# Strided attention heads as 72-token slices, two-bank MLP accumulators and reordered first transfers in a fused attention and MLP kernel

## The chip, the cores and the metric

The kernel runs on one core of a Trainium2 chip. The metric is the device time of one execution in microseconds; before the change the median of three runs is 445.27 us (444.51 to 446.03).

## The reference

Eight batches of attention with 8 heads over 576 tokens of 64 features, then an MLP on the 4608 tokens of 512 features:

```python
scores = scale * np.matmul(q, k.transpose(0, 1, 3, 2))
rel = pos[:, None] - pos[None, :]
mask_local = (rel >= 0) & (rel < stride)                       # heads 0 to 3, stride = 32
mask_strided = (rel >= 0) & (pos[None, :] % stride == pos[:, None] % stride)  # heads 4 to 7
...
attn = np.exp(scores)
attn = attn / (np.sum(attn, axis=-1, keepdims=True) + 1e-09)
...
x = np.ascontiguousarray(attn_out.transpose(0, 2, 1, 3)).reshape(B * S, H * D)
...
h = x @ w_in
sp = np.where(h > 20.0, h, np.log1p(np.exp(np.minimum(h, 20.0))))
g = h * np.tanh(sp)
return (g @ w_out).astype(np.float32)
```

A local head's token sees the 32 tokens up to itself; a strided head's token sees the tokens at distance 0, 32, 64 and so on behind it.

## The kernel before

Q, K and V come from HBM in float32 through one queue (SyncE's), are cast to bf16 (by GpSimd, for batch 0 partly by VectorE), and Q and K are transposed by TensorE, so that features lie on partitions (`t_steps`, L144: eight steps a batch, five transposes each, four of 128 tokens and one of 64). Scores are computed keys by queries: for local heads in windows of 96 queries against 128 keys (`qk_local`, L183), for strided heads in tiles of 7 residues of 18 tokens, 126 by 126, and a last one of 4 residues, 72 by 72 (`qk_str`, L203, `qk_str4`, L224). The copies behind the transposes put the strided tokens in residue order (L162, L166). ScalarE takes the exponential from PSUM into one of six tiles P, and GpSimd multiplies it with a mask (L197, L219, L238). The output steps (`pv_local`, `pv_str`) multiply P with V, to which a column of ones is appended, and VectorE divides by the sum that this column gives (`norm`, L243: a reciprocal and a product). The result is transposed back (`xt_local`, `xt_str`) into x^T, `xT`, which holds all 4608 tokens.

The MLP works in nine blocks of 512 tokens. Block t has a first half, `mlp1` (16 groups of four 512-column matmuls, each followed by Mish on ScalarE into gT), and a second half, `mlp2` (16 groups of four matmuls, four groups to each 128-token output tile; then a copy by VectorE and a store). A block's tokens lie in batch t and the batch before, so the attention of batch t + 1 is written in between the groups of block t: its transposes in the first half, its scores, outputs and x^T in the second, one step behind each group. All engines work in the order of the program; nothing is reordered later.

PSUM has eight banks: three single ones for MLP accumulators, a pair for scores, one for outputs, two for transposes. Loads, casts and attention of different batches overlap: at block t the program issues the casts of batch t + 2, then the loads of batch t + 3. On GpSimd the casts of batch t + 2 therefore stand ahead of the masks of batch t + 1 (L408 to L410 against L424). Each float32 landing tile exists once, so a load waits for the casts of the batch before it. The strided half of V is loaded by 20 transfers a batch, one per head and tile (L112 to L118). At the start SyncE issues K, Q, the constants and V of batch 0; w_in and w_out go through GpSimd's software queue, which casts to bf16 on the way.

Of the kernel before, what the change touches and what calls it, by code (L numbers as in the profile page):

```python
# [10 lines left out]
F32 = mybir.dt.float32  # L11
# [7 lines left out]
RG = 7  # L19
NA = 18  # L20
NTS = 5


def _masks():
    kk = np.arange(128)[:, None]
    qq = np.arange(WQ)[None, :]
    rel = qq + 32 - kk
    band = (rel >= 0) & (rel < STRIDE)
    loc = np.stack([band & (kk >= 32)] + [band] * (NW - 1), axis=1).astype(np.float32)

# [14 lines left out]
def kernel(ctx, tc, q, k, v, moe_w_in, moe_w_out, out):  # L45
# [19 lines left out]
    xT = const.tile([128, 4, NT], BF16, name="xT")  # L65
    loc = const.tile([128, NW, WQ], BF16, name="loc")
    m7 = const.tile([128, 126], BF16, name="m7")
    m4 = const.tile([128, 72], BF16, name="m4")
    ident = const.tile([128, 128], BF16, name="ident_sb")
    q32 = const.tile([128, 5, H, D], F32, name="q32")  # L70
    k32 = const.tile([128, 5, H, D], F32, name="k32")
    vl32 = const.tile([128, NW, 4, D], F32, name="vl32")
    vs32 = const.tile([128, NTS, 4, D], F32, name="vs32")
    qbf = [const.tile([128, 5, H, D], BF16, name=f"qbf{i}") for i in range(2)]
    kbf = [const.tile([128, 5, H, D], BF16, name=f"kbf{i}") for i in range(2)]
    vl = [const.tile([128, NW, 4, D + 1], BF16, name=f"vl{i}") for i in range(2)]
    vs = [const.tile([128, NTS, 4, D + 1], BF16, name=f"vs{i}") for i in range(2)]
    qTl = const.tile([128, 2, S], BF16, name="qTl")
    kTl = const.tile([128, 2, 32 + S], BF16, name="kTl")
    qTs = const.tile([128, 2, S], BF16, name="qTs")  # L80
    kTs = const.tile([128, 2, 640], BF16, name="kTs")
    NP = 6
    P = [const.tile([128, 2, 320], BF16, name=f"P{i}") for i in range(NP)]
    x_l = const.tile([128, NW, 256], BF16, name="x_l")
    x_s = const.tile([128, NTS, 256], BF16, name="x_s")
# [5 lines left out]
    ps_mm = ctx.enter_context(tc.tile_pool(name="psmm", bufs=3, space=PS))  # L91
    ps_s = ctx.enter_context(tc.tile_pool(name="pss", bufs=1, space=PS))
    ps_o = ctx.enter_context(tc.tile_pool(name="pso", bufs=1, space=PS))
    ps_t = ctx.enter_context(tc.tile_pool(name="pst", bufs=2, space=PS))


    def load_qk(b, dst, src):
        for kb in range(5):
            n = 128 if kb < 4 else 64
            nc.sync.dma_start(  # L100
                dst[0:n, kb, :, :],
                src[b, :, 128 * kb:128 * kb + n, :].rearrange("h p d -> p h d"),
            )
# [22 lines left out]
    def cast_qk(b, engs):  # L126
        for src, dst in ((q32, qbf[b % 2]), (k32, kbf[b % 2])):
            e = next(engs)
            cast(e, dst[:, 0:2, :, :], src[:, 0:2, :, :])
            cast(e, dst[:, 2:4, :, :], src[:, 2:4, :, :])  # L130
            cast(e, dst[0:64, 4, :, :], src[0:64, 4, :, :])

    def cast_v(b, engs):
        for i in range(0, NW, 3):
            cast(next(engs), vl[b % 2][:, i:i + 3, :, 0:D], vl32[:, i:i + 3, :, :])
        cast(next(engs), vs[b % 2][:, 0:4, :, 0:D], vs32[:, 0:4, :, :])
        cast(next(engs), vs[b % 2][0:72, 4, :, 0:D], vs32[0:72, 4, :, :])

    def forever(*es):
        while True:  # L140
            yield from es


    def t_steps(b):  # L144

        def step(which, hp):
            src = (qbf if which == "q" else kbf)[b % 2]
            tr = ps_t.tile([128, 1024], BF16, tag="tr", name="tr")
            for kb in range(5):
                n = 128 if kb < 4 else 64  # L150
                nc.tensor.transpose(  # L151
                    tr[:, 128 * kb:128 * kb + n],
                    src[0:n, kb, 2 * hp:2 * hp + 2, :],
                    ident[0:n, 0:n],
                )
            if hp < 2:
                dst = qTl[:, hp, :] if which == "q" else kTl[:, hp, 32:32 + S]
                nc.vector.tensor_copy(dst, tr[:, 0:S])
            else:
                dst = (qTs if which == "q" else kTs)[:, hp - 2, :]  # L160
                nat = tr[:, 0:S].rearrange("p (a r) -> p a r", r=32)
                nc.vector.tensor_copy(  # L162
                    dst[:, 0:504].rearrange("p (t a r) -> p t a r", t=4, r=RG),
                    nat[:, :, 0:28].rearrange("p a (t r) -> p t a r", r=RG),
                )
                nc.vector.tensor_copy(  # L166
                    dst[:, 504:576].rearrange("p (a r) -> p a r", r=4), nat[:, :, 28:32]
                )
        return [lambda w=w, hp=hp: step(w, hp) for hp in range(4) for w in ("k", "q")]

    pcount = [0]

    def attn_steps(b):
        Pof = {}
        vlb, vsb = vl[b % 2], vs[b % 2]
        tok0 = b * S

        def new_p():
            p = P[pcount[0] % NP]
            pcount[0] += 1  # L180
            return p

        def qk_local(hp, hf):  # L183
            ps = ps_s.tile([128, 2, 512], F32, tag="ps", name="ps")
            for w in range(3):
                i = 3 * hf + w
                for e in range(2):
                    nc.tensor.matmul(  # L188
                        ps[:, e, WQ * w:WQ * w + WQ],
                        lhsT=kTl[64 * e:64 * e + 64, hp, WQ * i:WQ * i + 128],  # L190
                        rhs=qTl[64 * e:64 * e + 64, hp, WQ * i:WQ * i + WQ],
                        start=True, stop=True,
                    )
            pt = new_p()
            nc.scalar.activation(pt[:, :, 0:288], ps[:, :, 0:288], AF.Exp, scale=scale)  # L195
            mk = loc[:, 3 * hf:3 * hf + 3, :].rearrange("p w c -> p (w c)")
            nc.gpsimd.tensor_tensor(  # L197
                out=pt[:, :, 0:288], in0=pt[:, :, 0:288],
# [256 lines left out]
```

## Time and profile before

| | |
|---|---|
| median of the runs | 445.27 us |
| profiled execution | 445.28 us, its span 443.2 us |
| TensorE, matmuls | 340.0 us busy (77%) |
| VectorE / ScalarE / GpSimd | 132.8 / 149.6 / 152.1 us busy |
| granted clock of TensorE, mean | 0.958 |
| DMA packets | 129,213, of which 120,352 under 512 bytes |
| bytes moved | 43.89 MB, 99 GB/s over the span |

The profile has a page of sums over the whole span, and views of the trace: sums by stretch, waits by who waited for whom, and a timeline by engine. Sums over the span mix stages here: TensorE's clock share in 40 slices falls below 9 tenths in the slices from about 100 to 155 us alone, and TensorE's busy share is low until there. So the reading goes by stages. Times on the timeline count from the span's start; the end of a matmul is modelled, so what one costs is read from the start of the next.

### The profile page before, as it was taken

What the parts mean: (1) busy time and instruction counts of PE and PEld (TensorE: products, weight loads), DVE (VectorE), ACT (ScalarE), POOL (GpSimd) and SP (SyncE); (2) the same over time, 40 slices, a digit from 0 to 9 for tenths busy, and PEclk for the clock granted to TensorE, in tenths of its full rate; (3) what the DMA queues carried; (4) which work ended last, traced back from release to release, by engine and by line L of the source; (5) the groups of instructions that cost most, each with busy time, mean ns of one, the idle gap of its engine ahead of it and who ended that gap; (6) DMA issues with size and microseconds to landing.
All of it is one profiled execution on the core that took longest, in us unless ns stands there. A gap on an engine that the chain in (4) does not pass through costs nothing.

```text
span 443.2 us, 6264 instructions
## 1 busy us (share of the span) xinstructions
PE 340.0 (77%) x2352; PEld 160.7 (36%) x2352; DVE 132.8 (30%) x422; ACT 149.6 (34%) x232; POOL 152.1 (34%) x204
## 2 busy tenths in 40 slices
PE   0050366940292598998999899899989999999996
PEld 0030132510141253444444344444534444444442
DVE  3140250200061122622552263245226324501001
ACT  1011222530030255245515524651553455160530
POOL 4010935123582105910960591096044009000000
PEclk9999999995597599999999999999999999999999
DMA  9961994492791891288159329812001001101101
GB/s 171 211 127 39 204 206 90 88 205 53 132 175 40 202 184 42 81 180 143 37 150 211 60 86 178 144 36 98 1 24 49 25 0 49 47 1 48 49 24 71
DMA packets 129213, 43.89 MB, mean 99 GB/s; under 512 B 120352, under 2 KB 124576, under 8 KB 129184
## 3 DMA queue, kind: packets, MB, share of 16 engines
q1 hardware_dynamic: 124960, 39.31, 43.7%
q0 software_dynamic: 4224, 4.19, 5.7%
q8 instruction: 18, 0.29, 0.3%
q14 instruction: 11, 0.09, 0.1%
HBM read 38.24 MB, written 9.44 MB: 108 GB/s over the span
## 4 chain that ended last, share of the span: by engine, by line
PE 62%; SPq 22%; DVE 4%; DMA 3%; ACT 3%; POOL 3%; issue 2%; POOLq 0%; ACTq 0%; DVEq 0%
PE psh L328 26%; PE pso L343 24%; SPq L115 13%; SPq L100 6%; PE tr L151 4%; PE po L256 3%; SPq L108 2%; ACT L195 2%; PE po L270 2%; DMA vs<-in_v_dram 1%; PE ps L188 1%; PE ps L208 1%; DMA q<-in_q_dram 1%; POOL P L197 1%; DVE osb L349 1%
## 5 line engine op out<-in xcount | busy, mean ns | idle before, releaser
L328 PE MATMUL psh<-xT,w_in 128*128 128x512 bf16 x576 | 140.7, 391 | 14.8 <-DVE xT L304 14.8
L343 PE MATMUL pso<-w_out,gT 128*128 128x512 bf16 x576 | 144.3, 381 | 0.0
L333 ACT ACTIVATE gT<-psh 128x512 bf16<-128x512 f32 x144 | 86.0, 597 | 158.1 <-PE psh L328 158.1
L197 POOL TENSOR_TENSOR P<-P,loc 128x576 bf16<-128x576 bf16 x32 | 39.8, 1278 | 133.1 <-ACT P L195 133.0
L328 PEld LDWEIGHTS <-w_in 128*128 128x128 bf16 x576 | 52.8, 99 | 75.5 <-issue 22.0
L343 PEld LDWEIGHTS <-gT 128*128 128x128 bf16 x576 | 48.8, 98 | 44.2 <-issue 1.0
L349 DVE COPY osb<-pso 128x512 f32<-128x512 f32 x36 | 24.9, 692 | 103.1 <-PE pso L343 90.8
L256 PE MATMUL po<-vl,P 128*128 128x65 bf16 x192 | 15.6, 204 | 42.3 <-POOL P L197 40.1
L151 PE MATMUL tr<-ident_sb,kbf 128*128 128x128 bf16 (+1 forms) x160 | 18.4, 229 | 28.8 <-DMA ident_sb<-ident 25.3
L215 ACT ACTIVATE P<-ps 128x504 bf16<-128x504 f32 x32 | 18.9, 591 | 63.5 <-PE ps L208 30.6
L219 POOL TENSOR_TENSOR P<-P,m 128x252 bf16<-128x252 bf16 x64 | 38.9, 637 | 2.2 <-ACT P L215 1.2
L245 DVE RECIPROCAL rden<-po 96x4 f32<-96x4 f32 (+2 forms) x88 | 15.5, 176 | 69.2 <-PE po L256 64.8
L195 ACT ACTIVATE P<-ps 128x576 bf16<-128x576 f32 x32 | 20.8, 651 | 42.0 <-PE ps L188 41.9
L151 PEld LDWEIGHTS <-kbf 128*128 128x128 bf16 (+1 forms) x160 | 13.2, 102 | 40.8 <-DVE qbf L379 20.7
L124 POOL CAST vs<-vs 128x1024 bf16<-128x1024 f32 (+1 forms) x16 | 11.3, 721 | 48.4 <-DMA vs<-in_v_dram 48.4
L256 PEld LDWEIGHTS <-P 128*128 128x128 bf16 x192 | 9.1, 102 | 48.1 <-POOL P L197 40.8
L124 POOL CAST qbf<-q 128x1024 bf16<-128x1024 f32 (+1 forms) x21 | 18.1, 896 | 17.8 <-DMA q<-in_q_dram 17.8
L246 DVE TENSOR_TENSOR x_l<-po,rden 96x256 bf16<-96x256 f32 x48 | 20.2, 420 | 1.7
L124 POOL CAST vl<-vl 128x768 bf16<-128x768 f32 x16 | 12.8, 826 | 22.5 <-DMA vl<-in_v_dram 22.5
L124 POOL CAST kbf<-k 128x1024 bf16<-128x1024 f32 (+1 forms) x21 | 18.1, 893 | 0.0
L188 PE MATMUL ps<-qTl,kTl 64*128 64x96 bf16 x192 | 10.2, 213 | 10.0 <-ACT P L195 10.0
L151 PE MATMUL tr<-ident_sb,qbf 128*128 128x128 bf16 (+1 forms) x160 | 17.6, 225 | 0.0
(41 smaller groups left out, 202.9 us busy)
## 6 DMA issues: line engine op xcount, KB each, us to landing
out_dram<-osb SPq DMA_DIRECT2D x36, 256.0 KB
k<-in_k_dram SPq DMA_DIRECT2D x32, 256.0 KB
q<-in_q_dram SPq DMA_DIRECT2D x32, 256.0 KB
vl<-in_v_dram SPq DMA_DIRECT2D x40, 128.0 KB
vs<-in_v_dram SPq DMA_DIRECT2D x128, 31.5 KB
w_in<-in_moe_w_in_dram POOLq DMA_DIRECT2D x4, 512.0 KB, 10.4
w_out<-in_moe_w_out_dram POOLq DMA_DIRECT2D x4, 512.0 KB, 12.0
k<-in_k_dram SPq DMA_DIRECT2D x8, 128.0 KB
```

Source lines behind the costliest of these rows:

```text
L100: nc.sync.dma_start(dst[0:n, kb, :, :], src[b, :, 128 * kb:128 * kb + n, :].rearrange("h p d -> p h d"),)
L115: nc.sync.dma_start(vs32[0:NA * nr, t, h, :], v[b, 4 + h].rearrange("(a r) d -> a r d", r=32)[:, RG * t:RG * t + nr, :],)
L124: eng.tensor_copy(out_, in_)
L151: nc.tensor.transpose(tr[:, 128 * kb:128 * kb + n], src[0:n, kb, 2 * hp:2 * hp + 2, :], ident[0:n, 0:n],)
L195: nc.scalar.activation(pt[:, :, 0:288], ps[:, :, 0:288], AF.Exp, scale=scale)
L197: nc.gpsimd.tensor_tensor(out=pt[:, :, 0:288], in0=pt[:, :, 0:288], in1=mk.unsqueeze(1).to_broadcast([128, 2, 288]), op=ALU.mult,)
L219: nc.gpsimd.tensor_tensor(out=pe, in0=pe, in1=m7.unsqueeze(1).to_broadcast([128, 2, 126]), op=ALU.mult,)
L256: nc.tensor.matmul(po[:, h, :], lhsT=pt[:, h % 2, WQ * w:WQ * w + 128], rhs=vlb[:, i, h, :], start=True, stop=True,)
L328: nc.tensor.matmul(ps[:], lhsT=w_in[:, cc, fc * 128:(fc + 1) * 128], rhs=xT[:, cc, 512 * t:512 * t + 512], start=(cc == 0), stop=(cc == 3),)
L333: nc.scalar.activation(gT[:, fc, :], ps[:], AF.Mish)
L343: nc.tensor.matmul(po[ot][:], lhsT=gT[:, fc, 128 * ot:128 * ot + 128], rhs=w_out[:, fc, :], start=(fc == 0), stop=(fc == 15),)
L349: nc.vector.tensor_copy(osb[:], po[ot][:])
```

## The change

Strided heads: the 576 tokens are put on 72 partitions of 8 consecutive tokens each (p, j), as they lie in memory. Token 8p + j meets in its row j only tokens with the same j, and among these the residue classes modulo 32 are p modulo 4; so each j is a slice of 72 by 72 with one mask, and nothing is put in residue order. There are 8 such slices a head, and 8 output steps a batch where there were 5. Local heads: 96 partitions of 6 consecutive tokens; the copy behind the transposes puts them in order. Strided Q and K are loaded by GpSimd's software queue straight to bf16, without a cast.

MLP accumulators are two tiles of two banks; Mish takes 1024 columns at a time. Output and transpose tiles share the two remaining banks. x^T is a ring of four batches, so block 4's matmuls are split in two. There are eight tiles P; three of the eight masks of a batch go to VectorE. Block 0 runs its second half with all four output tiles open.

The first transfers are issued strided Q and K first, local Q and K, then V; strided V is one transfer. In the loop, the casts of batch t + 2 and its following loads move behind the second half of block t.

```diff
@@ loads @@
+    def load_qk_str(b):
+        for dst, src in ((ks, k), (qs, q)):
+            nc.gpsimd.dma_start(
+                dst[b % 2][0:PN], src[b, 4:8].rearrange("h (p j) d -> p h (j d)", j=CS)
+            )
...
     def load_v(b):
+        nc.sync.dma_start(vs32[0:PN], v[b, 4:8].rearrange("h (p j) d -> p h j d", j=CS))
...
-        for t in range(NTS):
-            nr = RG if t < 4 else 4
-            for h in range(4):
-                nc.sync.dma_start(
-                    vs32[0:NA * nr, t, h, :],
-                    v[b, 4 + h].rearrange("(a r) d -> a r d", r=32)[:, RG * t:RG * t + nr, :],
-                )
@@ transposes @@
+        if kind == "s":
+            src = (qs if which == "q" else ks)[b % 2]
+            for u in range(8):
+                h, jj = 2 * hp + u // 4, u % 4
+                nc.tensor.transpose(
+                    tr[:, PN * u:PN * u + PN],
+                    src[0:PN, h, 128 * jj:128 * jj + 128],
+                    ident[0:PN, 0:PN],
+                )
+            cast(eng, (qTs if which == "q" else kTs)[:, S * hp:S * hp + S], tr[:, 0:S])
@@ scores, outputs, x^T @@
+                for u in range(4):
+                    c0 = PN * (4 * (2 * hp + hf) + u)
+                    for e in range(2):
+                        nc.tensor.matmul(
+                            ps[:, e, PN * u:PN * u + PN],
+                            lhsT=kTs[64 * e:64 * e + 64, c0:c0 + 128],
+                            rhs=qTs[64 * e:64 * e + 64, c0:c0 + PN],
...
+        def pv(self, kind, i):
+            po = tile_t("po")[:, 0:4 * (D + 1)].rearrange("p (h d) -> p h d", h=4)
...
+                dst = xT[:, 2:4, t0:t0 + S].rearrange("p c (n j) -> p c j n", j=CS)
+                cast(
+                    eng, dst[:, :, 4 * hf:4 * hf + 4, :],
+                    tr[:, 0:576].rearrange("p (c j n) -> p c j n", c=2, j=4),
+                )
...
+            [Q("s", 0, 0, Po)], [Q("s", 1, 0, Dv)], [Q("s", 0, 1, Po)], [Q("s", 1, 1, Dv)],
+            [Q("l", 0, 0, Po), V("s", 0)], [Q("l", 1, 0, Dv), V("s", 1)],
+            [Q("l", 0, 1, Po), V("s", 2), V("s", 3)], [Q("l", 1, 1, Po), V("s", 4)],
+            [V("s", 5), V("s", 6)], [V("s", 7), X("s", 0)], [V("l", 0), V("l", 1)],
+            [V("l", 2), X("s", 1)], [V("l", 3), V("l", 4)], [V("l", 5), X("l", 0)],
+            [X("l", 1)], [],
@@ MLP @@
+            ps = ps_mm.tile([128, 2, 512], F32, tag="mm", name="psh")
...
+            nc.scalar.activation(gT[:, 2 * g:2 * g + 2, :], ps[:], AF.Mish)
...
+        if fc_major:
+            order = [(ot, g4) for g4 in range(4) for ot in range(4)]
@@ opening @@
+        cast(Sc, vs[0][0:PN, :, :, 0:D], vs32[0:PN])
+        a.qk("s", 0, 0, Po)
+        a.qk("s", 1, 0, Dv, True)
...
+        cast_qk_loc(0, Dv, Po)
+        for i in range(0, NW, 3):
+            cast(Po, vl[0][:, i:i + 3, :, 0:D], vl32[:, i:i + 3, :, :])
@@ loop @@
-            if t + 2 < B:
-                cast_qk(t + 2, forever(nc.gpsimd))
-                cast_v(t + 2, forever(nc.gpsimd))
...
+            if t + 3 < B:
+                load_qk_str(t + 3)
+            for i, g in enumerate(mlp2(t, gT, fc_major=(t == 0))):
...
+            if t + 2 < B:
+                cast_qk_loc(t + 2, Po, Po)
+                cast_v(t + 2, Po, Po)
+            if t + 3 < B:
+                load_qk_loc(t + 3)
+                load_v(t + 3)
```

GpSimd's order between the attention of batch 0 and that of batch 1, before (batch 2's casts end here; `vs` is strided V, `P` the exponentials, `loc` the mask of local heads):

```order
L124 CAST qbf_69<-q_65 128x1024 x2
L124 CAST qbf_69<-q_65 64x512
L124 CAST kbf_71<-k_66 128x1024 x2
L124 CAST kbf_71<-k_66 64x512
L124 CAST vl_73<-vl_67 128x12x64 x2
L124 CAST vs_75<-vs_68 128x16x64
L124 CAST vs_75<-vs_68 72x4x64
L197 TENSOR_TENSOR P_84<-P_84,loc 128x2x288
L197 TENSOR_TENSOR P_85<-P_85,loc 128x2x288
```

and now (`stm` is the mask of strided heads, `ks` and `qs` their Q and K, `kl` and `ql` those of local heads):

```order
L101 DMA ks_75<-in_k_dram 72x4x512
L101 DMA qs_73<-in_q_dram 72x4x512
L204 TENSOR_TENSOR P_84<-P_84,stm 72x2x288
L204 TENSOR_TENSOR P_86<-P_86,stm 72x2x288
L204 TENSOR_TENSOR P_88<-P_88,loc 128x2x288
L204 TENSOR_TENSOR P_90<-P_90,loc 128x2x288
L204 TENSOR_TENSOR P_91<-P_91,loc 128x2x288
L125 CAST kl_70<-kl_67 96x4x6x64
L125 CAST ql_68<-ql_66 96x4x6x64
L125 CAST vs_78<-vs_65 72x32x64
L125 CAST vl_76<-vl_64 128x12x64 x2
```

The casts of batch 2 moved behind the masks of batch 1, and loads through the software queue now stand ahead of those masks.

SyncE's queue at the start, before (the loads of batch 0 and the constants; `m_62` and `m_63` are the masks of strided heads):

```order
L100 DMA k_66<-in_k_dram 128x8x64 x4
L100 DMA k_66<-in_k_dram 64x8x64
L100 DMA q_65<-in_q_dram 128x8x64 x4
L100 DMA q_65<-in_q_dram 64x8x64
L359 DMA ident_sb<-ident 128x128
L360 DMA loc<-locmask 128x576
L361 DMA m_62<-m7mask 128x126
L362 DMA m_63<-m4mask 128x72
L106 DMA vl_67<-in_v_dram 96x4x64
L108 DMA vl_67<-in_v_dram 128x4x64 x5
L115 DMA vs_68<-in_v_dram 126x1x64 x16
L115 DMA vs_68<-in_v_dram 72x1x64 x4
```

and now (strided Q and K stand at the head of GpSimd's queue):

```order
L323 DMA ident_sb<-ident 128x128
L324 DMA stm<-strmask 128x288
L107 DMA kl_67<-in_k_dram 96x4x384
L107 DMA ql_66<-in_q_dram 96x4x384
L326 DMA loc<-locmask 128x576
L113 DMA vs_65<-in_v_dram 72x4x512
L114 DMA vl_64<-in_v_dram 96x4x64
L116 DMA vl_64<-in_v_dram 128x4x64 x5
```

The 20 transfers of strided V became one, which stands ahead of local V, and the transposes' identity moved from behind ten loads to the front.

VectorE from the last transposes of the first half of block 1 into its second half, before:

```order
L162 COPY qTs<-tr 128x504
L166 COPY qTs<-tr 128x72
L349 COPY osb<-pso 128x512
L245 RECIPROCAL rden<-po 96x4
L246 TENSOR_TENSOR x_l<-po,rden 96x256
```

and now:

```order
L125 COPY qTl<-tr 128x576
L204 TENSOR_TENSOR P_85<-P_85,stm 72x2x288
L311 COPY osb<-pso 128x512
L204 TENSOR_TENSOR P_87<-P_87,stm 72x2x288
L226 RECIPROCAL rden<-po 72x4
L227 TENSOR_TENSOR x_s<-po,rden 72x256
L204 TENSOR_TENSOR P_89<-P_89,loc 128x2x288
```

Three masks a batch now stand on VectorE, between the output copies and the normalisations.

## Rows read from the trace of the kernel before

**Rows 1.** Sums by stretch: stretch, length, busy us by engine, granted clock, DMA share, GB/s

```profile
0.00:63.18 63.18, 15.19 (x150) 9.57 (x151) 18.87 (x60) 7.94 (x11) 21.65 (x36) 1.00 0.90 158
63.18:135.56 72.38, 42.91 (x280) 18.92 (x280) 15.15 (x53) 17.50 (x27) 33.56 (x42) 0.83 0.70 123
135.56:188.70 53.14, 39.47 (x281) 18.33 (x280) 15.40 (x50) 17.50 (x27) 18.83 (x25) 0.87 0.51 112
227.68:266.64 38.96, 37.36 (x281) 17.78 (x280) 15.39 (x50) 17.50 (x27) 18.55 (x25) 1.00 0.64 123
383.50:443.20 59.70, 55.62 (x259) 24.98 (x257) 6.43 (x11) 19.12 (x32) 0.00 (x0) 1.00 0.11 40
```

**Rows 2.** Waits from 0 to 150 us: waiter <- releaser: total, times, longest

```profile
POOL vs L124 <- DMA vs<-in_v_dram: 48.4, 8, 11.7
...
PE po L256 <- POOL P L197: 40.1, 4, 23.8
```

**Rows 3.** Timeline of SyncE's queue: start, us, what, count

```profile
23.60 2.95 SPq L108 DMA_DIRECT2D vl<-in_v_dram  x5
26.67 16.25 SPq L115 DMA_DIRECT2D vs<-in_v_dram  x20
```

**Rows 4.** Timeline in block 0, GpSimd and TensorE; in brackets the idle time before

```profile
116.77 4.96 POOL L197 TENSOR_TENSOR P<-P,loc 128x576 bf16<-128x576 bf16 x4
...
118.09 0.29 PE L256 MATMUL po<-vl,P 128*128 128x65 bf16 x2 [23.80 <-POOL P L197]
```

**Rows 5.** Timeline of TensorE in a steady block

```profile
230.40 1.90 PE L328 MATMUL psh<-xT,w_in 128*128 128x512 bf16 x8
232.13 0.52 PE L151 MATMUL tr<-ident_sb,qbf 128*128 128x128 bf16 x5
...
249.07 0.30 PE L188 MATMUL ps<-qTl,kTl 64*128 64x96 bf16 x6 [1.11 <-ACT P L195]
...
252.81 0.29 PE L208 MATMUL ps<-qTs,kTs 64*128 64x126 bf16 x4
253.03 0.30 PE L256 MATMUL po<-vl,P 128*128 128x65 bf16 x4
253.17 1.02 PE L343 MATMUL pso<-w_out,gT 128*128 128x512 bf16 x4
...
259.25 0.42 PE L281 MATMUL tr<-ident_sb,x_l 96*128 96x96 bf16 x6
259.50 0.29 PE L270 MATMUL po<-vs,P 126*128 126x65 bf16 x4
...
266.57 0.23 PE L297 MATMUL tr<-ident_sb,x_s 72*128 72x72 bf16 x2
266.64 0.59 PE L328 MATMUL psh<-xT,w_in 128*128 128x512 bf16 x2
```

**Rows 6.** Sums by stretch, the start of block 1 after its wait

```profile
148.70:153.00 4.30, 4.30 (x14) 1.65 (x14) 0.46 (x1) 1.19 (x2) 0.00 (x0) 0.50 0.97 218
```

**Rows 7.** Groups by line and form: count, busy us, mean ns, idle before

```profile
L333 ACT ACTIVATE gT<-psh 128x512 bf16<-128x512 f32 x144 | 86.0, 597 | 158.1 <-PE psh L328 158.1
L197 POOL TENSOR_TENSOR P<-P,loc 128x576 bf16<-128x576 bf16 x32 | 39.8, 1278 | 133.1 <-ACT P L195 133.0
```

**Rows 8.** Timeline of VectorE in the opening

```profile
4.04 0.43 DVE L376 CAST kbf<-k 128x512 bf16<-128x512 f32 x1 [1.02 <-DMA k<-in_k_dram]
5.25 0.68 DVE L376 CAST kbf<-k 128x512 bf16<-128x512 f32 x1 [0.78 <-DMA k<-in_k_dram]
```

**Rows 9.** Timeline of VectorE in a steady block

```profile
262.58 0.17 DVE L245 RECIPROCAL rden<-po 126x4 f32<-126x4 f32 x1
...
263.13 0.45 DVE L286 COPY xT<-tr 128x576 bf16<-128x576 bf16 x1
```

**Rows 10.** Sums by stretch: w_in beside other loads; V's transfers alone

```profile
7.00:18.00 11.00, 0.00 (x0) 0.00 (x0) 0.54 (x2) 0.00 (x0) 0.00 (x0) 1.00 1.22 196
30.00:42.00 12.00, 2.57 (x32) 1.51 (x30) 1.40 (x6) 2.60 (x4) 0.47 (x1) 1.00 0.17 39
```

More of the change, by code (lines that the diff above doesn't have):

```diff
@@ L18 @@
 WQ = 96
-RG = 7
-NA = 18
-NTS = 5
+CL, PL = 6, 96
+CS, PN = 8, 72
+RING = 4
 def _masks():
@@ L139, in forever @@
-    def forever(*es):
-        while True:
-            yield from es
-    def t_steps(b):
[L146 to L158, printed above, removed]
-            else:
[L160 to L169, printed above, removed]
@@ L256, in pv_local @@
                 nc.tensor.matmul(
[L257 removed]
+                    po[:, h, :], lhsT=pt[0:n, c0:c0 + 128], rhs=rhs,
                     start=True, stop=True,
                 )
[L260 to L274 removed]
@@ L309, in attn_steps @@
[L309 to L319 removed]
+            dst = (x_l if kind == "l" else x_s)[0:m, i, :]
@@ L322, in mlp1, with segs @@
+    def segs(t):
+        a, e, o, r = 512 * t, 512 * t + 512, 0, []
+        while a < e:
+            n = min(e - a, RT - a % RT)
+            r.append((a % RT, n, o))
+            a, o = a + n, o + n
+        return r
     def mlp1(t):
         gT = g_pool.tile([128, 16, 512], BF16, tag="gT", name="gT")
-        def group(fc):
-            ps = ps_mm.tile([128, 512], F32, tag="mm", name="psh")
-            for cc in range(4):
-                nc.tensor.matmul(
-                    ps[:], lhsT=w_in[:, cc, fc * 128:(fc + 1) * 128],
-                    rhs=xT[:, cc, 512 * t:512 * t + 512],
-                    start=(cc == 0), stop=(cc == 3),
-                )
-            nc.scalar.activation(gT[:, fc, :], ps[:], AF.Mish)
@@ L334, in mlp1, with group @@
-        return gT, [lambda fc=fc: group(fc) for fc in range(16)]
-    def mlp2(t, gT):
+        def group(g):
+            ps = ps_mm.tile([128, 2, 512], F32, tag="mm", name="psh")
+            for u in range(2):
+                fc = 2 * g + u
+                for a, n, o in segs(t):
+                    for cc in range(4):
+                        nc.tensor.matmul(
+                            ps[:, u, o:o + n], lhsT=w_in[:, cc, fc * 128:(fc + 1) * 128],
+                            rhs=xT[:, cc, a:a + n], start=(cc == 0), stop=(cc == 3),
+                        )
+            nc.scalar.activation(gT[:, 2 * g:2 * g + 2, :], ps[:], AF.Mish)
@@ L337, in mlp2 @@
+        return gT, [lambda g=g: group(g) for g in range(8)]
+    def mlp2(t, gT, fc_major=False):
         po = {}
         def group(ot, g4):
-            if g4 == 0:
-                po[ot] = ps_mm.tile([128, 512], F32, tag="mm", name="pso")
+            if ot // 2 not in po:
+                po[ot // 2] = ps_mm.tile([128, 2, 512], F32, tag="mm", name="pso")
+            p = po[ot // 2]
             for fc in range(4 * g4, 4 * g4 + 4):
                 nc.tensor.matmul(
-                    po[ot][:], lhsT=gT[:, fc, 128 * ot:128 * ot + 128], rhs=w_out[:, fc, :],
+                    p[:, ot % 2, :], lhsT=gT[:, fc, 128 * ot:128 * ot + 128], rhs=w_out[:, fc, :],
@@ L390 @@
             )
[L391 to L402 removed]
+        cast_qk_loc(1, Po, Po)
+        cast_v(1, Po, Po)
+        load_qk_str(2)
+        load_qk_loc(2)
         load_v(2)
```

388 lines of the change are left out of this document (172 added, 216 removed).

## The prediction

> **What bounds the kernel now.** I read the spans by stage first [rows 1]. The core's span is 443.2 us, and 2.1 us lie around it (the profiled execution took 445.28 us; the median of the runs is 445.27 us, so the sum can be made against this execution). Nine MLP blocks follow an opening. The opening takes 63.2 us, block 0 takes 72.4 us and block 1 53.1 us, yet blocks 2 to 6 take 38.96 us each, and the last two with the tail 59.7 us. In a steady block TensorE is busy 37.4 of 38.96 us; in block 0 it is busy 42.9 of 72.4. So there are two regimes: TensorE sets the pace from 188.7 us on, and something else before.
>
> The waits of the first 150 us tell what [rows 2]: GpSimd stood 48.4 us waiting for the strided half of V, and TensorE 40.1 us waiting for GpSimd's masks. The queue of SyncE shows why the data is late [rows 3]: one batch's strided V is 20 transfers, and issuing them takes 16.2 us, 0.8 us apiece. Meanwhile the DMA engines are 17% busy (the window 30 to 42 us [rows 10]), so the issue is the limit there, not the bytes. A late V hurts more than it must, because GpSimd takes the casts of batch 2 ahead of the masks of batch 1: the masks start at 116.77 us, and TensorE has waited 23.8 us when the first is done [rows 4].
>
> **The change part by part: the opening.** SyncE issues 9 transfers a batch where it issued 36, and GpSimd's queue 2. At 0.6 us (the local V) to 0.8 us each [rows 3] that is 5 to 7 us a batch on SyncE in place of 22 to 29; the issue stops being the limit and the bytes take over. Until the strided V has landed, the queues write 0.6 MB of strided Q and K (now bf16), 1.2 MB of local Q and K, 0.25 MB of constants, 0.6 MB of V and, interleaved from the other queue, I take 0.5 MB of w_in: 3.1 MB. At the 196 GB/s of the window in which w_in and other loads ran together [rows 10] that is 16 us, and the strided V is there at about 17 us if the start costs 2 us (the first K was used at 4.04 us, after transfers of its own [rows 8]); somewhat earlier if the two queues fill the engines better than that; I take 16. Everything of batch 0 and w_in, 5.4 MB, is in by 29 us.
>
> From 16 us a chain runs: ScalarE's cast of V (2048 wide; 597 ns for 512 [rows 7], so 2.4 us) stands in front of the exponentials; four exponentials at 0.65 us end at 21; a mask on VectorE and its cast of the local K (1536 wide at 0.43 us for 512 [rows 8], 1.3 us) reach 23; four transposes with copies 24.5; four more exponentials 27; eight strided outputs at 0.55 us of VectorE each 31.4. GpSimd comes in at the same point: its casts of the local V wait for the last bytes (28 to 29 us), then two masks of 1.28 us [rows 7] reach about 31.5. Six local outputs (3.3 us) and the last transposes and copy (0.9 us) give the first MLP matmul at **36 us** instead of 63.2. Bounds: 32 us if V lands at 12 us, 45 us if the queues deliver at half the rate.
>
> **Blocks 0 and 1.** What stalled them is removed twice over: the V of batch 2 is there earlier, and GpSimd now takes the masks of batch 1 before the casts of batch 2 (the piece of its order in the section on the change). What is late next could be w_out (issued at about 32 us; 2.1 MB beside as much of batches 1 and 2 are 21 us at 196 GB/s, so it is in by about 53 us; the second half of block 0 starts at about 54 us and takes w_out quarter by quarter), so I count no stall. Block 0 still starts TensorE at the granted clock of 0.50 for some 4.3 us, as block 1 did before [rows 6], and half of that is lost: 2.2 us. Its four copies of the MLP output all fall at its end (all four accumulators stay open): 1 us. Block 0 is a steady block plus 3.2 us, block 1 a steady block.
>
> **A steady block**, from TensorE's own rows [rows 5]. The first half has 64 MLP matmuls at 0.216 us (eight from 230.40 to 232.13), 13.82 us, and now 32 transposes of 72 columns at 0.033 us (two of this shape lie between 266.57 and 266.64) and 24 of 96 columns at 0.0425 us (six from 259.25 to 259.50): 2.08 us. Sum 15.9 us. The second half has the same 13.82 us; eight score steps at 0.33 us (0.22 us from 252.81 to 253.03, and 0.1 us between the MLP matmuls before it and it) make 2.64; 14 output steps where there were 11, at 0.135 us (253.03 to 253.17), make 1.89; the transposes of x 1.04. The wait of 1.1 us for the first exponential (249.07; ScalarE reloads its table first) stays, I take 1.3. Sum 20.7 us.
>
> To this come waits for VectorE, which has more to do: 14 normalisations at 0.55 us (the next operation starts 0.55 us after a reciprocal, 262.58 to 263.13 [rows 9]) are 7.7 us where 11 were 6.05, three masks are new, and the copies of x^T fall from 16 pieces to four of 576 columns. From step 5 to step 13 VectorE has about 10.6 us of work (13 normalisations 7.2, a mask 0.4, two output copies 1.2, three copies of x^T 1.8) beside 11.3 us of TensorE's, and an output tile and a transpose tile now share two PSUM buffers. Two tiles in one step then make TensorE wait a little. Going through the steps with these durations I find five waits of 0.15 to 0.55 us, 1.6 us in all. A mask on VectorE and a copy with a stride in its output are not in the trace. For the mask, the nearest rows are 0.43 us (the cast of 512) and 1.28 us (the same mask on GpSimd); I take 0.45, since VectorE's cast is the nearer. A strided copy I take at 0.75. The bounds of the waits are 0 (all covered) and 4 us (three masks at 1.28 us and what queues behind them). Nothing else takes their place: ScalarE's 1024-wide pass is at most twice 597 ns [rows 7], 1.2 us, against 1.73 us of matmuls in a group, so two accumulator pairs suffice; GpSimd has about 15 us of work. The wait of 0.4 us for the last x^T at a block's start goes. In block 4 the split at the ring's end doubles the matmuls at half the columns and costs nothing I can price.
>
> Steady block: 15.9 + 20.7 + 1.6 = 38.2, and 0.2 for what I missed: **38.4 us** against 38.96.
>
> **The sum.** 36 + 7 x 38.4 (268.8) + 3.2 + 55.2 (four half blocks at 13.8) + 3.7 for the last copy and store = 366.9 us of span, and 2.1 around it: **369 us**. By stage the gain of 76 us is 27 in the opening, 31 in block 0, 15 in block 1 and 3 in all the rest.
>
> [...] VectorE's cast of one shape took 0.43 us at 4.04 us and 0.68 us at 5.25 us [rows 8]. The masks on VectorE may thus run longer beside GpSimd's work than alone; that is part of rival A. [...]
>
> [...]
>
> **The rivals.**
> A. *The steady block gets longer.* VectorE becomes the limit of the second half, because the masks wait for GpSimd or the strided copies are slow. For it: 10.6 against 11.3 us leaves no room; against it: the masks fall where VectorE is mostly idle. One mask in three delayed by 1.28 us and the normalisations behind it give 39.5 to 41 us a block: 377 to 387 us.
> B. *The transfers still bind the opening.* The software queue carries strided Q and K, w_in and w_out; the local V queues beside them packet by packet. For it: 196 GB/s is all that both queues gave together; against: 3.1 MB are needed early and the order is by need. With 45 us of opening and 5 to 10 us of stall in block 0 the time is 383 to 388 us.
> C. *The order does not do what it says.* The opening stays at 60 us, because the small transfers wait for each other as before: 393 us.
> D. *Better than forecast.* No VectorE waits and 33 us of opening: 355 to 360 us.
> E. *Slower than before.* GpSimd's queue is in order, and the software loads of batch t+3 now stand in front of the masks of batch t+1. If such an issue waits for an earlier transfer in every block, as the masks waited 23 us for V in block 0, all seven blocks pay. It decides from 76/7 = 10.9 us a block; at 23 us a block the time is 530 us. Against it: the loads are issued two blocks ahead of their use, and a batch needs some 15 us of transfer in 38 us.
>
> **How the numbers follow.** Forecast (364 to 375 us) 0.60, A 0.15, B 0.10, C 0.04, D 0.08, E 0.03. The range of 358 to 388 us holds the forecast, A, B and the upper half of D, a little over 8 in 10 after allowing for what is not on the list. What a measurement of this kernel can tell from no change is 0.3%, 1.3 us; every case but E is far beyond it: faster 0.96, the same 0.01, slower 0.03.
>
> **What would show it.** Right: the first MLP matmul at 32 to 40 us; no wait of GpSimd for V longer than a few us after the opening; blocks 0 to 6 within 2 us of each other, but for the slow clock in block 0; steady blocks of 38 to 39 us with waits for VectorE under 0.6 us each. A wait of TensorE for VectorE over 1 us in every block is A; TensorE waiting for a DMA in the first half of block 0, or for w_out, is B; a GpSimd issue that ends a wait of the masks is E. I am wrong in the main point if blocks 0 and 1 still lose over 20 us together.

## The result: 424.5 us, and the profile after

The changed kernel takes 424.49 us (median of four runs, 423.23 to 426.21) against 445.65 us for the kernel before in the same comparison: a ratio of 0.953 (95% interval 0.949 to 0.957). The forecast was 369, with a range of 358 to 388. The direction is right, the size is not: a gain of 21 us in place of 76.

Sums by stretch of the changed kernel, in the columns of [rows 1]: opening, blocks 0, 1 and 2, last two blocks and tail.

```profile
0.00:46.92 46.92, 15.28 (x196) 11.35 (x197) 21.57 (x53) 17.34 (x18) 23.48 (x27) 1.00 1.11 204
46.92:94.40 47.48, 41.87 (x325) 20.47 (x325) 21.44 (x46) 15.95 (x18) 16.20 (x15) 0.93 0.57 114
94.40:138.90 44.50, 38.91 (x326) 19.55 (x325) 22.61 (x47) 14.67 (x17) 14.02 (x12) 0.92 0.46 100
138.90:183.29 44.39, 38.92 (x326) 19.53 (x324) 22.60 (x47) 15.84 (x18) 14.04 (x12) 0.92 0.48 95
361.00:424.40 63.40, 55.85 (x256) 24.73 (x253) 6.06 (x9) 17.56 (x17) 0.00 (x0) 1.00 0.10 38
```

The opening, block 0 and block 1 are 16, 25 and 9 us shorter than before; a steady block is 5.4 us longer (44.4 against 38.96), at a mean granted clock of 0.92 where it was 1.00, and the last two blocks with the tail are 4 us longer (they begin at 360.63). The next view shows what TensorE waited for, in the form of [rows 2] (total, times, longest):

```profile
PE po L220 <- DVE rden L226: 19.8, 14, 1.8
...
PE pso L305 <- DVE osb L311: 9.4, 18, 0.8
...
PE po L220 <- ACT xT L123: 4.8, 3, 2.3
```

No mask stands among the releasers any more (the 40.1 us of [rows 2] are gone). VectorE's reciprocals take their place: each of seven blocks has two long waits. One of them is put down to the copy itself, and one of the 14 counted here, of 0.6 us, lies in the opening. The timelines of VectorE and of TensorE in block 3 show them; they answer to [rows 9] and [rows 5]:

```profile
214.72 2.71 DVE L125 COPY xT<-trx 128x576 bf16<-128x576 bf16 x1
217.06 0.37 DVE L226 RECIPROCAL rden<-po 96x4 f32<-96x4 f32 x1
...
219.83 2.70 DVE L125 COPY xT<-trx 128x576 bf16<-128x576 bf16 x1
...
225.47 0.45 DVE L125 COPY xT<-trx 128x576 bf16<-128x576 bf16 x1
```

```profile
217.49 0.29 PE L220 MATMUL po<-vl,P 128*128 128x65 bf16 x4 [1.82 <-DVE rden L226]
217.61 1.02 PE L305 MATMUL pso<-w_out,gT 128*128 128x512 bf16 x4
218.47 0.29 PE L220 MATMUL po<-vl,P 128*128 128x65 bf16 x4
...
219.42 1.86 PE L305 MATMUL pso<-w_out,gT 128*128 128x512 bf16 x4 [0.39 <-DVE osb L311]
221.08 0.42 PE L220 MATMUL po<-vl,P 128*128 128x65 bf16 x4
222.58 0.38 PE L220 MATMUL po<-vl,P 128*128 128x65 bf16 x4 [1.07 <-DVE rden L226]
```

The first two x^T copies are the strided heads' (`xt`, L251): 2.7 us each; the local heads' copy of as many elements takes 0.45. Behind each, TensorE waits for a normalisation. After the first wait four MLP matmuls still take 0.86 us (217.61 to 218.47); the next four take 1.66 (219.42 to 221.08), so the clock has fallen before the third wait. The sum of that stretch has the clock in its third column from the end:

```profile
219.05:225.88 6.83, 5.39 (x28) 2.64 (x28) 5.38 (x11) 0.00 (x0) 1.00 (x2) 0.50 0.10 38
```

The granted clock is 0.50 for these 6.8 us, and for as long in every steady block of the changed kernel. In the opening the same copy stands on ScalarE (first view) and holds the local outputs (second). VectorE's masks, 0.46 to 0.59 us each in the loop, take 4.01 us for two beside GpSimd's (third):

```profile
36.40 5.28 ACT L123 COPY xT<-trx 128x576 bf16<-128x576 bf16 x2 [6.20 <-PE trx L240]
```

```profile
39.17 0.38 PE L220 MATMUL po<-vl,P 128*128 128x65 bf16 x4 [2.26 <-ACT xT L123]
41.73 0.60 PE L220 MATMUL po<-vl,P 128*128 128x65 bf16 x8 [2.18 <-ACT xT L123]
```

```profile
19.71 4.01 DVE L204 TENSOR_TENSOR P<-P,stm 72x576 bf16<-72x576 bf16 x2 [4.99 <-ACT P L203]
```

### The profile page after: what moved, and what is told of

Same layout as the page of the kernel before. It is cut to its first block, busy times and chain, and to the rows that moved or that the text cites. A ratio compares the mean times of both kernels' runs of the same rounds, so it can differ in the third digit from the quotient of the medians.

```text
span 424.4 us, 6633 instructions
## 1 busy us (share of the span) xinstructions
PE 346.7 (82%) x2784; PEld 180.2 (42%) x2784; DVE 184.8 (44%) x390; ACT 144.7 (34%) x160; POOL 114.7 (27%) x105
## 4 chain that ended last, share of the span: by engine, by line
PE 63%; DVE 21%; ACT 8%; issue 4%; DMA 3%; SPq 1%; ACTq 0%
PE psh L290 28%; PE pso L305 25%; DVE xT L125 9%; DVE x_s L227 3%; DMA vs<-in_v_dram 3%; PE po L220 3%; DVE osb L311 3%; ACT P L203 3%; DVE P L204 2%; PE tr L154 2%; ACT L294 2%; PE trx L240 2%; DVE rden L226 2%; ACT gT L294 1%; ACT xT L123 1%
## 5 line engine op out<-in xcount | busy, mean ns | idle before, releaser
L305 PE MATMUL pso<-w_out,gT 128*128 128x512 bf16 x576 | 158.6, 408 | 9.4 <-DVE osb L311 9.4
L290 PE MATMUL psh<-xT,w_in 128*128 128x512 bf16 (+1 forms) x640 | 135.9, 362 | 2.2 <-ACT gT L294 1.7
L294 ACT ACTIVATE gT<-psh 128x1024 bf16<-128x1024 f32 x72 | 73.1, 1024 | 91.2 <-PE psh L290 91.2
L203 ACT ACTIVATE P<-ps 72x576 bf16<-72x576 f32 (+1 forms) x64 | 41.0, 649 | 36.4 <-PE ps L185 25.7
L204 POOL TENSOR_TENSOR P<-P,stm 72x576 bf16<-72x576 bf16 x16 | 20.2, 1266 | 121.8 <-ACT P L203 121.8
L220 PEld LDWEIGHTS <-P 72*128 72x128 bf16 (+1 forms) x448 | 27.0, 108 | 51.9 <-issue 34.8
L125 DVE COPY xT<-trx 128x576 bf16<-128x576 bf16 x29 | 44.6, 1538 | 6.0 <-PE trx L240 6.0
L226 DVE RECIPROCAL rden<-po 72x4 f32<-72x4 f32 (+1 forms) x112 | 22.0, 196 | 22.7 <-PE po L220 22.6
L227 DVE TENSOR_TENSOR x_s<-po,rden 72x256 bf16<-72x256 f32 x64 | 26.9, 421 | 2.2
L220 PE MATMUL po<-vs,P 72*128 72x65 bf16 x256 | 18.6, 202 | 5.2 <-DVE x_s L227 4.7
## 6 DMA issues: line engine op xcount, KB each, us to landing
vl<-in_v_dram SPq DMA_DIRECT2D x40, 128.0 KB, 10.9
```

What stands on the lines that cost most here:

```text
L125: eng.tensor_copy(out_, in_)
L203: nc.scalar.activation(pt[0:n, :, 0:288], ps[0:n, :, 0:288], AF.Exp, scale=scale)
L204: meng.tensor_tensor(out=pt[0:n, :, 0:288], in0=pt[0:n, :, 0:288], in1=mk.rearrange("p w c -> p (w c)").unsqueeze(1).to_broadcast([n, 2, 2 ...
L220: nc.tensor.matmul(po[:, h, :], lhsT=pt[0:n, c0:c0 + 128], rhs=rhs, start=True, stop=True,)
L226: nc.vector.reciprocal(rden[0:m, :], po[0:m, :, D])
L227: nc.vector.tensor_tensor(out=dst.rearrange("p (h d) -> p h d", h=4), in0=po[0:m, :, 0:D], in1=rden[0:m, :].unsqueeze(2).to_broadcast([m, ...
```

## The experiments

The theory to test is that the copy that writes every eighth column (16 bytes apart) costs 2.7 us and holds VectorE's normalisations, and that the waits cost TensorE its clock besides. Every ratio below is to the kernel before, with its 95% interval.

**e1: each copy takes one half of the features and all eight rows, and writes its columns in order.** The first copy stands one step later, since it needs all eight outputs; in the opening both stand among the local outputs.

```diff
...
-                    eng, dst[:, :, 4 * hf:4 * hf + 4, :],
-                    tr[:, 0:576].rearrange("p (c j n) -> p c j n", c=2, j=4),
+                    eng, xT[:, 2 + hf, t0:t0 + S].rearrange("p (n j) -> p n j", j=CS),
+                    tr[:, 0:S].rearrange("p (j n) -> p n j", j=CS),
...
```

> One part undone: each strided x^T copy takes one feature half with all eight rows j, so that it writes its 576 columns one after another and reads PSUM with a step, in place of writing every eighth column; the first such copy stands one step later, since it needs all eight outputs. Copy theory (the copy that writes every eighth column lasts 2.7 us in place of 0.75, holds the normalisations back, and TensorE's wait behind them costs it the full clock): the copy lasts 0.7 to 0.9 us on VectorE and about as long on ScalarE, the waits of the output steps go below 0.5 us a block, the granted clock stays at 1.00, the steady block comes from 44.4 to 38.5 to 40 us, the first MLP matmul from 46.9 to 42 to 44 us, and the whole to 378 to 388 us. [...] Rival, VectorE has too much to do with eight more normalisations: the block gains only the copy's own 3.8 us if VectorE sets the pace, the clock still drops, and the whole is 395 to 405.

The time is 384.91 us, a ratio of 0.865 (0.863 to 0.868). The views show the opening and a steady block (sums by stretch), and a copy (timeline):

```profile
0.00:41.98 41.98, 15.23 (x197) 11.35 (x198) 19.92 (x53) 13.34 (x18) 22.30 (x26) 1.00 1.10 203
...
160.99:200.30 39.31, 36.56 (x326) 18.67 (x325) 18.87 (x47) 15.84 (x18) 14.03 (x12) 1.00 0.51 107
```

```profile
193.65 0.76 DVE L125 COPY xT<-trx 128x576 bf16<-128x576 bf16 x1 [0.44 <-PE trx L250]
```

The copy takes 0.76 us, the clock stays at 1.00, the block takes 39.3 us and the opening 42.0: as the copy theory said.

**e5: e1 with the copy's loops exchanged again**, with the same transposes at the same place: `"p (n j) -> p j n"` on both sides.

> The kernel of run e1 with one thing turned back: the strided copy goes through the same 576 elements with the same transposes at the same place, but row j by row j, so that it writes every eighth column and reads one element after another. Copy theory: the order of writing alone makes the cost, so the copy is back at 2.6 to 2.8 us, the clock falls again, and the time goes from 385 to 418 to 430 us. Rival, the new transposes (eight of one half in place of four of both) or the later place brought the gain: the time stays below 395.

The time is 425.81 us, a ratio of 0.956 (0.953 to 0.960). The copies take 2.69 to 2.73 us, the opening 46.4, and the block 44.6 at a clock of 0.92 (sum by stretch, timeline):

```profile
138.40:182.99 44.59, 39.13 (x325) 19.61 (x324) 22.61 (x47) 15.83 (x18) 14.03 (x12) 0.92 0.49 95
```

```profile
175.32 2.69 DVE L125 COPY xT<-trx 128x576 bf16<-128x576 bf16 x1
```

The order in which the copy goes through its elements alone makes the difference of 41 us. It turns reading and writing at once; e7 takes them apart.

**e8: only the first of the two copies in the slow order.**

> The kernel of run e1 with one of the two copies a batch in the slow order, the first. If a wait costs only itself, half of the 5 us a block between run e1 and the changed kernel: 41.8 us a block and 403 to 407 in all. If the drop of the clock is what makes it dear, and one wait of under 2 us does not bring it about, the clock stays at 1.00 and the block at 40 to 41.2: 390 to 400.

The time is 405.10 us, a ratio of 0.910 (0.906 to 0.913). Three blocks, the first of them block 0:

```profile
43.85:87.95 44.10, 39.62 (x324) 19.54 (x324) 19.64 (x46) 15.95 (x18) 16.21 (x15) 0.96 0.70 138
87.95:129.08 41.13, 36.51 (x325) 18.57 (x324) 20.76 (x47) 14.67 (x17) 14.05 (x12) 1.00 0.51 108
129.08:170.27 41.19, 36.68 (x326) 18.64 (x324) 20.75 (x47) 15.84 (x18) 14.05 (x12) 1.00 0.52 103
```

Neither line of the expectation held as a whole: the time is that of the first, but the clock stays at 1.00 in four of the seven blocks (1, 2, 3 and 6). There one copy costs 1.9 us (41.2 - 39.3), its wait. In blocks 0, 4 and 5 the clock fell too, to a mean of 0.96, and they took 44.1, 42.8 and 42.2 us. Up to the fall, blocks 4 and 5 have the same waits for VectorE as the blocks at 1.00 (1.82 us, then 0.2), so the waits alone do not tell when it falls; what does is not shown. The second copy costs 3.4 us more (44.6 in e5 - 41.2): its own wait of 1.07 us is one part, the lower clock another. As an estimate, the 5.39 us of TensorE's work in the 6.8 us above would be 2.7 us less at the full clock; the two parts were not measured apart.

**e3: the two copies on ScalarE**, as they stand: `a.xt(kd, hf, nc.scalar if kd == "s" else None)`.

> The two strided x^T copies of a batch go to ScalarE in the loop, which has no exponential or Mish to do at their place; layout and all else as in the changed kernel. Copy theory: they last 2.65 us there as in the opening, but hold nobody's normalisation: the waits on VectorE's reciprocals go, the clock stays at 1.00 or falls for less than 2 us a block, the block comes to 39 to 40.5 us and the whole to 382 to 395. Rival, the transpose tiles are the bound (two banks for outputs and transposes, one of them held for the copy's whole 2.65 us): TensorE waits as long as before, now for ScalarE, and the time stays above 412.

The time is 417.27 us, a ratio of 0.938 (0.933 to 0.943). The rival was right. The copies last 2.7 us there too, and TensorE waits for them (waits):

```profile
PE po L220 <- ACT xT L123: 24.7, 17, 2.3
```

Outputs and transposes share two PSUM tiles; one is held for the whole copy of 2.7 us, whoever makes it. So the queue of VectorE is only one way in which the copy holds TensorE.

**e2: all masks of the loop on GpSimd.**

> All eight masks of a batch on GpSimd in the loop, as before the change; the opening and all copies as in the changed kernel. Masks rival (VectorE's masks and GpSimd's hold each other up): the strided copies fall below 1.5 us, the block from 44.4 to 40 to 42 us, the whole to 395 to 410. Copy theory: the copies stay at 2.6 to 2.7 us, since no mask stands beside them; three masks of 0.45 to 0.6 us leave VectorE early in the second half, where it isn't late, and GpSimd's row of eight masks may hold the first outputs: 422 to 432 us, 1 or 2 us either way.

The time is 425.74 us, a ratio of 0.957 (0.954 to 0.959). The copies take 2.69 and 2.71 us and the block 44.7, so VectorE's masks cost the loop of this kernel nothing that can be measured. With a fast copy this was not tried.

**e7: 19 copies of 576 columns at the end of e1**, when the kernel's own work is done (one execution, each copy once).

> The kernel of run e1 with 19 copies of 576 columns more at its end, when nothing else runs: on VectorE and ScalarE from PSUM, writing bf16 every 1st, 2nd, 4th or 8th column, and float32 every 1st, 2nd, 4th or 7th; on VectorE and GpSimd from SBUF, writing every 1st or 8th column, and one that reads every 8th. If the step of the writes makes the cost, a float32 copy with a step of 16 bytes is as slow as a bf16 one with 16 bytes (2.7 us) and it grows with the step; if the 2-byte writes make it (several to one stretch of memory, written apart), float32 with any step stays below 0.9 us and bf16 is slow from a step of two on. Reading with a step costs 0.9 us or less in both.

These are the eight on VectorE from PSUM: four to bf16, writing every 1st, 2nd, 4th and 8th column, and four to float32, writing every 1st, 2nd, 4th and 7th (timeline).

```profile
379.34 0.45 DVE L422 COPY wr<-src 128x576 bf16<-128x576 bf16 x1
379.82 0.80 DVE L423 COPY wr<-src 128x576 bf16<-128x576 bf16 x1
380.65 1.43 DVE L424 COPY wr<-src 128x576 bf16<-128x576 bf16 x1
382.12 2.70 DVE L425 COPY wr<-src 128x576 bf16<-128x576 bf16 x1
384.45 0.96 DVE L426 CAST wr<-src 128x576 f32<-128x576 bf16 x1
385.44 0.76 DVE L427 CAST wr<-src 128x576 f32<-128x576 bf16 x1
386.23 1.17 DVE L428 CAST wr<-src 128x576 f32<-128x576 bf16 x1
387.43 1.18 DVE L429 CAST wr<-src 128x576 f32<-128x576 bf16 x1
```

Neither line of the expectation holds whole. In bf16 the time nearly doubles with each doubling of the step, though the reading is in order in all four; float32 at the same 16 bytes takes 1.17 us, and more bytes add nothing. ScalarE is nearly the same (0.64, 0.80, 1.43, 2.70), and GpSimd from SBUF is as slow (0.66 in order and 2.73 at every 8th, on 96 partitions). VectorE from SBUF is faster (0.31 and 1.45 on 96 partitions, beside two of ScalarE's copies). Reading every 8th column on VectorE took 0.67. Why two-byte writes suffer more, and why less from SBUF on VectorE, is left open.

**e4: the kernel before with the order of the loop alone**: casts of batch t + 2 and loads behind block t's second half.

> The kernel before with one part of the change alone: the casts of batch t + 2 and the loads that follow them stand behind the second half of block t. Theory of the stall (masks of batch t + 1 stood behind casts that waited for transfers): block 0 loses its wait of 23.8 us and block 1 its own of 16, about 31 and 15 us by stage as predicted, so 395 to 405 us in all. Rival, the transfers bind anyway (20 issues of strided V a batch keep the queue late): the waits come back at the casts and masks one block later and the whole stays above 425. Both leave the opening at 63 us and the steady block at 39.

The time is 415.89 us, a ratio of 0.935 (0.932 to 0.937): above the 395 to 405 expected and below the rival's 425. Blocks 0 and 1:

```profile
64.16:110.40 46.24, 41.13 (x280) 18.49 (x280) 15.06 (x53) 17.50 (x27) 25.34 (x32) 1.00 0.66 119
110.40:158.85 48.45, 39.83 (x281) 18.45 (x280) 15.40 (x50) 17.50 (x27) 18.82 (x25) 0.89 0.54 119
```

Block 0 loses its stall (72.4 to 46.2 us, [rows 1]), block 1 only 4.7 of the 15 us expected: part of the time comes back there as a wait of 7.4 us for x^T. With 29 us the order alone gains more than the whole change did (21).

**e6: e1 with three things mended that its trace still shows.** Output tiles 0 and 2 share an accumulator, and 1 and 3 the other; the tables of the exponential and of Mish are loaded early; in the opening, the transposes of local Q and K go ahead of the strided scores, and the casts of local V behind all masks. The first two in the code:

```diff
...
-            if ot // 2 not in po:
+            if ot % 2 not in po:
...
+            if at:
+                Sc.preload_act_table(AF.Exp)
...
+                if at and i == 7:
+                    Sc.preload_act_table(AF.Mish)
...
```

> The kernel of run e1 with what its trace still shows: (1) in the opening the casts and transposes of local Q and K stand ahead of the strided scores and the casts of local V behind all masks; (2) the tables of the exponential and of Mish are loaded as soon as ScalarE is done with the other; (3) output tiles 0 and 2 share one two-bank accumulator, 1 and 3 the other, so that a tile's first matmul does not wait for the copy of the one before. Theory: the first MLP matmul comes from 42.0 to 36 to 38.5 us; of a steady block's 39.3 us the waits of 0.20 (Mish), 1.11 (first exponential) and 0.54 and 0.16 (copy of the output tile) go, for 37.5 to 38.3; in all 385 - 4.5 - 8 x 1.3 = 366 to 374 us. Rival, the waits come back behind the next late step (the exponentials' own 0.65 us, or the masks): the block stays above 38.8 and the whole at 377 to 381.

The time is 368.82 us, a ratio of 0.828 (0.826 to 0.830). A steady block:

```profile
117.24:155.12 37.88, 36.17 (x325) 18.36 (x324) 18.78 (x47) 15.94 (x18) 14.03 (x12) 1.00 0.54 112
```

The block came as expected, the opening (39.98) not. VectorE's two strided masks, 5.76 us together, end only when GpSimd is done with its masks (27.00) and a cast of 0.82 us; its two local ones follow (timelines of GpSimd and of VectorE):

```profile
21.84 2.71 POOL L204 TENSOR_TENSOR P<-P,stm 72x576 bf16<-72x576 bf16 x2 [8.82 <-ACT P L203]
24.51 2.49 POOL L204 TENSOR_TENSOR P<-P,loc 128x576 bf16<-128x576 bf16 x2
```

```profile
22.32 5.76 DVE L204 TENSOR_TENSOR P<-P,stm 72x576 bf16<-72x576 bf16 x2 [3.27 <-ACT P L203]
28.01 0.81 DVE L204 TENSOR_TENSOR P<-P,loc 128x576 bf16<-128x576 bf16 x2
```

**e10 and e9: the opening's masks all on VectorE; in e9 also the cast of strided V on GpSimd.**

> The kernel of run e6 with all eight masks of the opening on VectorE. In run e6 two of VectorE's masks take 5.76 us together, from 22.32 to 28.08, and end 1 us after GpSimd's last one. Theory, the two engines take turns, and a mask of VectorE waits until GpSimd's masks and casts leave a gap: without GpSimd's masks each lasts 0.40 to 0.50 us behind its exponential, the last ends at 26 to 27 us, and the first MLP matmul comes from 40.0 to 37.5 to 39; the whole to 366 to 368 us. Rival, VectorE's masks are slow in the opening for another reason (first touch of the mask or of P): they stay above 1 us each, eight of them end after 30, and the first MLP matmul is at 40 or later.

> As run e10, and the cast of strided V of batch 0 on GpSimd in place of ScalarE, where it stands 1.9 us ahead of the first exponential. Theory: the exponentials start 1.5 to 1.9 us earlier, the outputs follow, and the first MLP matmul comes to 36 to 37.5 us, the whole to 364 to 366. Rival, the cast on GpSimd (1.9 us, while VectorE copies the last transposes) holds VectorE, or the outputs wait for local V, whose last transfer lands at 28.5 to 30: no more than 0.5 us below run e10.

VectorE's masks in e10:

```profile
21.45 2.06 DVE L204 TENSOR_TENSOR P<-P,stm 72x576 bf16<-72x576 bf16 x4 [2.73 <-ACT P L203]
23.60 2.07 DVE L204 TENSOR_TENSOR P<-P,loc 128x576 bf16<-128x576 bf16 x4
```

They take about 0.5 us each, and the first MLP matmul comes at 36.8 us in e10 and 35.2 in e9, earlier than either expectation said. Yet the times are 367.98 us (0.825, 0.820 to 0.829) and 367.89 us (0.826, 0.823 to 0.830), the same as e6: block 0 grows from 39.4 to 44.1 us in both and ends at 80.92 in e10 and 79.35 in e9, where it ended at 79.36 in e6. In e9 GpSimd's cast of local V waits for a transfer, the masks stand behind it, and TensorE waits for them (timelines of GpSimd and TensorE):

```profile
56.28 0.83 POOL L125 CAST vl<-vl 128x768 bf16<-128x768 f32 x1 [8.37 <-DMA vl<-in_v_dram]
...
60.00 2.67 POOL L204 TENSOR_TENSOR P<-P,stm 72x576 bf16<-72x576 bf16 x2
```

```profile
61.49 0.20 PE L220 MATMUL po<-vs,P 72*128 72x65 bf16 x1 [1.62 <-POOL P L204]
62.72 0.27 PE L220 MATMUL po<-vs,P 72*128 72x65 bf16 x3 [1.03 <-POOL P L204]
```

**e11: e9 with those casts behind the masks of batch 1. e12: e6 with the loop's order of before.**

> The kernel of run e9 with GpSimd's casts of local V of batch 1 behind the masks of batch 1 in block 0, and the load of batch 2's V behind them. In run e9 the first MLP matmul came to 35.2 us as expected, but block 0 grew from 39.4 to 44.1 us: the second of these casts waits 8.4 us for a transfer that lands at 56 whatever the opening does, and the masks stand behind it. Theory, that cast alone holds the masks: the waits of 1.62 and 1.03 us for GpSimd's masks go, the clock stays at 1.00, block 0 comes to 39 to 40 us, and the whole to 362 to 365 us. Rival, the transfers bind block 0 anyway (w_out's last quarter, strided Q and K of batch 2 or local V of batch 1, all queued by then): something else waits for them, block 0 stays above 42 and the whole at 366 to 369.

> The kernel of run e6 with one part of the change turned back: the casts of batch t + 2 and the loads behind them stand ahead of block t, as before the change. Theory: the masks of batch 1 stand again behind casts that wait for batch 2's transfers, which start when the casts of batch 1 are done (47 and 57 us) and need some 10 us; so block 0 waits 8 to 13 us for its masks, partly at the lower clock, later blocks little: 378 to 388 us. Rival, strided V in one transfer and 49 thousand packets in place of 129 make the loads early enough by themselves: 368 to 372.

e11 takes 363.50 us, a ratio of 0.816 (0.813 to 0.818). Its block 0 takes 39.9 us (35.02 to 74.96) at the full clock, and the time is 61 us below the changed kernel's, the lowest of all runs. e12 takes 381.94 us, 0.857 (0.854 to 0.860): block 0 takes 55.3 us, since it waits for its masks, and no later block is longer than in e6.

```profile
77.21 0.24 PE L220 MATMUL po<-vs,P 72*128 72x65 bf16 x1 [12.54 <-POOL P L204]
```

## Why the prediction was wrong

The profiled span is 424.4 us, the sum was 366.9. The 57.5 us lie so: opening 10.9 (46.9 against 36), block 0 5.9, blocks 1 to 6 35.8, the last two and the tail 4.9. The slow copy makes 42 of them; 15 are left in e1, which has no slow copy (382.1): 6.0 in the opening, 5.4 in blocks 1 to 6 and 4.9 in the last two, less 1.1 in block 0.

**"A strided copy I take at 0.75."** This step failed. The copy measured 2.7 us. Between e1 and e5, which differ in its order alone, lie 42.4 us of span: 4.5 in the opening, 6.7 in block 0 and 31.3 in blocks 1 to 6. The prediction had bounds for the masks and none for this copy. The trace of before has copies into x^T that write with gaps, in runs of 7 neighbouring columns (or 4) with the next run 32 columns on; four of them, 504 columns, took 0.66 us (timeline of VectorE):

```profile
264.69 0.66 DVE L304 COPY xT<-tr 128x126 bf16<-128x126 bf16 x4 [0.45 <-PE tr L297]
```

None writes single columns apart, so the nearest rows gave 0.75 us no warning, and the term needed a long bound for that reason. Rival A named the mechanism, but at 39.5 to 41 us a block it was priced from the masks, so its time ended at 387 us. The sign that the prediction named for A, a wait for VectorE of over 1 us in every block, is what the profile shows.

**The waits.** The "five waits of 0.15 to 0.55 us, 1.6 us in all" are about right without the slow copy: e1 has five for VectorE in a steady block, 0.16 to 0.54 us, 1.4 in all. With it the longest were 1.82, 1.07 and 0.39. That the clock can be low after a wait was read from block 1 of before (0.50 for 4.3 us [rows 6]), but not counted for a wait made by the change.

**Two smaller waits not seen in the diff.** Two output tiles share one accumulator, and a matmul into it waits for VectorE's copy of the tile before, though the two use different halves of it. In the last two blocks these waits are 0.78 us (timeline of TensorE in the changed kernel):

```profile
379.73 7.07 PE L305 MATMUL pso<-w_out,gT 128*128 128x512 bf16 x32 [0.78 <-DVE osb L311]
387.58 3.61 PE L305 MATMUL pso<-w_out,gT 128*128 128x512 bf16 x16 [0.78 <-DVE osb L311]
```

And from block 2 on the table of Mish is loaded only when the first group of matmuls is done (timeline of ScalarE):

```profile
185.10 1.28 ACT L294 ACT_TABLE_LOAD   x1 [16.98 <-PE psh L290]
186.39 1.94 ACT L294 ACTIVATE gT<-psh 128x1024 bf16<-128x1024 f32 x2
```

With both mended, and the exponential's table loaded early as well (its wait falls from 1.11 to 0.74 us a block), e6 takes 14 us less than e1 in span after the opening: 1.1 in block 0, 8.3 in blocks 1 to 6, 4.7 in the last two. All three were changed in one run; how the gain divides among them is not shown.

**What held.** The strided V is used at 16.7 us (forecast 16). Blocks 0 and 1 lose their stall; e4 and e12 show the order of casts and masks as the cause, at 29 and 13 us. The slow clock counted at the start of block 0 (2.2 us) did not come: e1's block 0 has a granted clock of 1.00. A steady block without the slow copy takes 39.3 us (e1) where the sum said 38.4. In e6 it takes 37.9, and the first half of it 15.9 (117.24 to 133.14), just as the sum had for TensorE's own work there. That e6's span of 366.0 us comes so near to the 366.9 of the sum is luck in part: e6 has changes that the sum did not count on, its opening is 4.0 us longer than forecast, and block 0 and blocks 1 to 6 are 2.2 and 2.9 us shorter.

**The opening's masks.** The sum had one mask on VectorE's path, and together with a cast it gave it 2 us (21 to 23). Beside GpSimd's masks two took 5.76 us together (e6), and alone four took 2.06 (e10); between these two runs the opening falls from 39.98 to 36.8 us. So one of the two in e6 took 2.9 us or more, longer than any one operation of GpSimd there (2.71 us for two masks, 2.49 for two more, 0.82 for a cast). That it waited through several of them is an estimate from these times; what held it is not shown. In the loop of the changed kernel, e2 shows no cost.

**Rivals.** A was the right kind: its second condition, the slow strided copies, came true, and its first, masks that wait for GpSimd, only in the opening. B came true in small, and not in the changed kernel: once the opening was short, a transfer held block 0 through a cast (e9), until the order was changed (e11). C, D and E did not occur.

## What to carry to other kernels

Before a layout moves a permutation into a copy, look at which side is written with a step: here the same copy cost 2.7 us written with a step and 0.76 us read with one. An operation that no row shows needs a long bound of its own, and a wait in a TensorE-bound stage has to be priced with the lower clock that may follow it (here 0.50 for 6.8 us a block). When a stage gets shorter and the end of the next stands still, look for a queue in which work that is ready stands behind work that waits for a transfer.

## What was not expected of the hardware

From PSUM, the cost of a step in two-byte writes is the same on VectorE and ScalarE (e7): 4.7 ns an element at 16 bytes (2.70 us for 576), 1.4 ns at 4 bytes (0.80 us). Float32 written in order (0.96 us) was slower than with a step of two (0.76) in the one pair measured on VectorE. Two masks on VectorE took 5.76 us together beside a row of GpSimd's operations without a gap (e6), where four alone took 2.06 (e10). With one wait of 1.82 us in a block the clock stayed at 1.00 in four of e8's seven blocks and fell in three; in blocks 1 to 6 of the changed kernel, with waits of 1.82 and 0.39 us, it fell every time (a mean of 0.92 in each), in the one shown before the third wait came.
